# Loading attention inputs four heads at a time, spreading the loads over a group's steps, and reordering the last output tiles

## The chip, the cores and the metric

The kernel runs on one core of one Trainium2 chip, in one launch. The metric is the device time of that launch in microseconds (us), as the median of several runs. One further execution was taken with the hardware profiler; all rows below are from it.

## The reference, cut to what matters

Inputs are float32: local queries, keys and values of 4 batches, 8 heads, 512 positions and head size 64, and 32 global rows per head. Global rows attend to everything; a local row attends to the 32 global rows and to local rows at most 32 positions away. Two feed-forward nets over 2176 tokens follow.

```python
k_all = concat([k_g, k_l], axis=2); v_all = concat([v_g, v_l], axis=2)
out_g = sm(scale * q_g @ k_all.T) @ v_all
s_ll  = where(abs(pos[:, None] - pos[None, :]) <= 32, scale * q_l @ k_l.T, -1e9)
out_l = sm(concat([scale * q_l @ k_g.T, s_ll])) @ v_all
x = concat([out_g, out_l], axis=2)           # to [2176, 512]
h = x @ w_in;  x = (h * cos(h)) @ w_out      # 512 -> 2048 -> 512
h = relu(x @ w2_in);  out = (h * h) @ w2_out
```

## The kernel before, in words

**Attention.** Heads are taken in pairs, pair p from 0 to 15 (four pairs to a batch). Two pairs make a group of four heads, group gi from 0 to 7. A group is five items: two halves of 256 rows for each of its two pairs (class Local, line 400) and the 128 global rows of its four heads (class Global, line 526). There are 40 items, and the program is written by hand as a pipeline of steps (the loop at line 896). In step s item s has its scores made on TensorE (`S`, lines 405 and 530), its softmax on VectorE and ScalarE (`SM`, lines 421 and 546), one step later its reciprocal and normalisation (`RC`, `NM`), two steps later the transposes of its weights (`TM`, lines 476 and 591), and at lags 3 and 4 their evacuation and the product with the values (`TE`, `OM`, lines 483, 492, 606). Within a step the stages are emitted in the order of `CFG["order"]` (line 26); `CFG["lag"]` (line 28) says how many steps behind its item each is.

Before an item can start, its pair's keys and queries are transposed on TensorE: `TRK` (line 321) three steps ahead, `TRQ` (line 359) two steps ahead. `KEV` (line 334, ScalarE) and `KC` (line 348, GpSimd) evacuate and copy the keys. The last 32 keys of all heads are loaded once as `ktn`, transposed at `prep_ktail` (line 380), and copied in by `KC`.

**Loads.** Every load is issued by hand on the SyncE queue (SP in the rows), except the first queries and `ktn`, which ScalarE issues (lines 630 to 635). Per pair there are four transfers of keys (`load_k`, line 265), two of queries (`load_q`, line 280), five of values (`load_v`, line 290, into the ring `VA`), and two that copy the values, shifted by 64 rows, from `VA` to `VB` within SBUF (`copy_v`, line 307). In DRAM each row of a head is 64 floats, so these loads consist of 256-byte pieces. `LK`, `LQ`, `LV` and `CV` in the order place them for pair p + 2. Queue instructions run in order: one that must wait for a tile holds up all behind it. In `OM` the first product with `VB` waits for the second copy.

**Weights.** The float32 weights are split into a high and a low part. `Feed` (line 164) loads a block of 512 KB on SP (`conv_load`, line 119), and three, four and five steps later ScalarE, VectorE and GpSimd each do a part of the conversion (`conv_a`, `conv_b`, `conv_c`). A credit of 0.35 per step in which it is allowed paces it; in attention it starts a block at steps 3, 8, 13 and so on, five steps apart.

**Feed-forward.** `ffn_step` (line 856) makes one block of 128 hidden features for up to 512 tokens per step: three products per pair of operands (high by high, low by high, high by low), first into `h` (`g1`, line 746), then three steps later into `y` (`g2`, line 764). Sums over groups of hidden blocks are kept in `ypart`. In the last group of the second net `y_evac` (line 784) adds `y` and `ypart` into a fresh tile `osb` of two buffers, and `store` (line 804) writes it out: one transfer for a tile of local rows, four for the tile of global rows, which is the very last one.

```python
            elif c in ("LK", "LQ", "LV", "CV"):
                p = due(L[c])
                if p is not None and p + 2 < B * NPAIR:
                    dict(LK=load_k, LQ=load_q, LV=load_v, CV=copy_v)[c](p + 2)
```

Of the kernel before, what the change touches and what calls it, by code (L numbers as in the profile page):

```python
# [40 lines left out]
         'LK': -2,  # L41
         'LQ': 0,
         'LV': 3,
         'CV': 6},
# [18 lines left out]
def kernel(  # L63
# [100 lines left out]
    class Feed:  # L164


        def __init__(self):
            self.jobs = [(g, q) for g in range(2 * NC) for q in range(2)]
            self.stage = [None] * 6
            self.credit = 0.0  # L170
            self.nsplit = 0
            self.done = 0
            self.half = None

        def begin(self, rate):

            self.credit = min(self.credit + rate, 2.0)
            job = None
            if self.credit >= 1.0 and self.jobs:
                g, q = self.jobs[0]  # L180
                if g < self.nsplit + NR:
                    job = self.jobs.pop(0)
                    conv_load(*job)
                    self.credit -= 1.0
            self.stage = [job] + self.stage[:-1]
            a, b, c = self.stage[3:]
            if a:
                conv_a(*a)
            return conv_b(*b) if b else []

        def end(self):
            c = self.stage[5]
            if c:
                conv_c(*c)
                self.done += 1
# [59 lines left out]
    VA = [lp.tile([P, 5, 2, D], F32, name=f"va{i}") for i in range(4)]  # L255
    VB = [lp.tile([P, 4, 2, D], F32, name=f"vb{i}") for i in range(4)]
# [8 lines left out]
    def load_k(p):  # L265
        b, kk = divmod(p, NPAIR)
        h0 = 2 * kk
        t = ep.tile([P, 4, 2, D], F32, tag="kn", name="kn", bufs=2)
        nc.sync.dma_start(t[0:SG, 0], k_g[b, h0 : h0 + 2].rearrange("h p d -> p h d"))
        nc.sync.dma_start(  # L270
            t[SG:P, 0], k_l[b, h0 : h0 + 2, 0 : P - SG].rearrange("h p d -> p h d")
        )
        kn[p] = t
        for h in range(2):
            nc.sync.dma_start(
                t[:, 1:4, h],
                k_l[b, h0 + h, P - SG : SL - SG].rearrange("(c p) d -> p c d", p=P),
            )

    def load_q(p, queue=nc.sync):  # L280
        b, kk = divmod(p, NPAIR)
        h0 = 2 * kk
        u = ep.tile([P, 4, 2, D], F32, tag="qn", name="qn", bufs=2)
        for h in range(2):
            queue.dma_start(
                u[:, :, h], q_l[b, h0 + h].rearrange("(c p) d -> p c d", p=P)
            )
        qn[p] = u

    def load_v(p):  # L290
        b, kk = divmod(p, NPAIR)
        h0 = 2 * kk
        va = VA[p % 4]
        nc.sync.dma_start(va[0:32, 0], v_g[b, h0 : h0 + 2].rearrange("h p d -> p h d"))
        nc.sync.dma_start(
            va[32:128, 0], v_l[b, h0 : h0 + 2, 0:96].rearrange("h p d -> p h d")
        )
        for h in range(2):
            nc.sync.dma_start(  # L299
                va[:, 1:4, h],  # L300
                v_l[b, h0 + h, 96:480].rearrange("(c p) d -> p c d", p=P),
            )
        nc.sync.dma_start(
            va[0:32, 4], v_l[b, h0 : h0 + 2, 480:512].rearrange("h p d -> p h d")
        )

    def copy_v(p):
        va, vb = VA[p % 4], VB[p % 4]
        nc.sync.dma_start(vb[0:64], va[64:128, 0:4])
        nc.sync.dma_start(vb[64:128], va[0:64, 1:5])  # L310
# [10 lines left out]
    def tr_k(p):  # L321
        b, kk = divmod(p, NPAIR)
        tk = bank(BT, "tk")
        for c in range(4):
            nc.tensor.transpose(  # L325
                tk[:, c * P : (c + 1) * P],
                kn[p][:, c].rearrange("p h d -> p (h d)"),
                ident,
            )
        t = ep.tile([P, 8, KTB], F32, tag="kT", name="kT", bufs=3)  # L330
        kT[p] = t
        tks[p] = tk
# [15 lines left out]
    def k_copy(p):  # L348
        b, kk = divmod(p, NPAIR)
# [7 lines left out]
        nc.gpsimd.tensor_scalar(t[:, 7, 64:128], ktail[:, kk, b, :], **one)  # L357

    def tr_q(p):
        tq = bank(BT, "tq")  # L360
        for c in range(4):
            nc.tensor.transpose(  # L362
                tq[:, c * P : (c + 1) * P],
                qn[p][:, c].rearrange("p h d -> p (h d)"),
                ident,
            )
# [33 lines left out]
    class Local:  # L400
# [91 lines left out]
        def o_mm(self):  # L492
            self.o = bank(BO, "o")[:, 0:256].rearrange("p (i q) -> p i q", i=2)
            for i in range(2):
# [9 lines left out]
                for half in range(2):  # L504
                    v = (VB if half else VA)[self.p % 4]
                    q = slice(64 * half, 64 * half + 64)
                    for h in range(2):
                        nc.tensor.matmul(  # L508
                            self.o[64 * h : 64 * h + 64, i, q],
                            lhsT=v[:, 2 * self.hb + i, h, :],  # L510
# [15 lines left out]
    class Global:  # L526
# [79 lines left out]
        def o_mm(self):  # L606
            self.o = bank(BO, "og")[:, 0 : 2 * SG].rearrange("p (i q) -> p i q", i=2)
            for i in range(2):
                va = VA[(self.b * NPAIR + 2 * self.g + i) % 4]
                for c in range(5):  # L610
                    for h in range(2):
# [4 lines left out]
                            lhsT=va[0:r, c, h, :],  # L616
# [13 lines left out]
    load_q(0, nc.scalar)  # L630
    load_k(0)
# [4 lines left out]
    load_k(1)  # L636
    load_q(1)
# [125 lines left out]

    def g2(s):
# [3 lines left out]
        ne = NK if net == 0 else n // P  # L768
        if c_first:
            yps[:] = [bank(BY, "y") for e in range(ne)]  # L770
        for e in range(ne):
# [12 lines left out]
    def y_evac(s):  # L784
        net, first, last, (c0, n), _, _, _ = steps[s]
        for e, y in enumerate(yps):
# [17 lines left out]
    def store(t, osb):  # L804
        if t * P < NLOC:
            b, j = divmod(t * P, SL)
            r0 = b * (SL + SG) + SG + j
            nc.sync.dma_start(out[r0 : r0 + P, :], osb)
        else:
            for b in range(B):  # L810
                r0 = b * (SL + SG)
                nc.sync.dma_start(out[r0 : r0 + SG, :], osb[SG * b : SG * b + SG, :])
# [83 lines left out]
    for s in range(L["TRK"], NI + L["OE"]):  # L896
        due = lambda k: due_tr.get(s - k)
        cb, qe = [], []
        for c in CFG["order"]:
# [7 lines left out]
            elif c in ("TRK", "TRQ", "KEV", "KC", "QE"):  # L907
# [21 lines left out]
            elif c in ("LK", "LQ", "LV", "CV"):  # L929
                p = due(L[c])  # L930
                if p is not None and p + 2 < B * NPAIR:
                    dict(LK=load_k, LQ=load_q, LV=load_v, CV=copy_v)[c](p + 2)
            else:
# [3 lines left out]
                if c == "S":  # L937
                    i.s_mm()
                    if s == 0:
                        small = prep_qg()  # L940
                elif c == "SM":
                    for op in i.softmax():
                        op()
                    if s == 0:
# [5 lines left out]
                else:  # L950
                    dict(NM=i.norm, TM=i.t_mm, TE=i.t_evac, OM=i.o_mm, OE=i.o_evac)[c]()
        if s == 0:
            load_v(1)
        if s == 1:
            copy_v(1)
# [13 lines left out]
    open_pool("y", "o", "w2")  # L969
# [40 lines left out]
```

## Time and profile before

| what | value |
|---|---|
| median of 3 runs (lowest to highest) | 923.08 us (921.78 to 923.24) |
| the profiled execution: its time | 922.14 us |
| its span, first to last instruction | 920.4 us |
| TensorE (PE) busy | 888.4 us, 97% of the span |
| VectorE (DVE) / ScalarE (ACT) / GpSimd (POOL) busy | 489.8 / 473.3 / 407.1 us |
| moved by DMA | 57.09 MB |

The span lies 1.7 us below the time of its own execution, which lies 0.9 us below the median. "Idle before" in a row is the time for which an engine stood still ahead of an instruction, and the name behind the arrow is what ended it. PEclk is the granted TensorE clock as a share of full speed (1.0 is the 2.4 GHz level, 0.5 the 1.2 GHz level).

### The profile page before, as it was taken

The page shows a single profiled execution, that of the slowest core. Times are in us where ns is not written, and L with a number is a line of the kernel's source. Part 1 is how long each engine was busy: PE and PEld are TensorE (multiplying, and loading weights), DVE is VectorE, ACT ScalarE, POOL GpSimd, SP SyncE. Part 2 cuts the span into 40 slices and gives each one's busy share as a digit, 9 for nine tenths or more (in the row PEclk, how much of TensorE's full clock was granted, in tenths as well). Part 3 has the DMA queues.
Part 4 walks back from the last instruction along what each step waited for, and adds up shares of the span by engine and source line. Part 5 has one row for each costly group of instructions (what it writes and reads, how often), then busy time and mean ns, then how long its engine had stood idle before and what let it go on. Part 6 is the DMA issues. An engine that isn't in the chain of part 4 may idle for free.

```text
span 920.4 us, 15407 instructions
## 1 busy us (share of the span) xinstructions
PE 888.4 (97%) x5696; PEld 792.5 (86%) x5696; DVE 489.8 (53%) x1049; ACT 473.3 (51%) x1096; POOL 407.1 (44%) x458
## 2 busy tenths in 40 slices
PE   4898989999999999999999999999999999999997
PEld 3677767999999999999999988888989888889995
DVE  3666868667767566864565484433423733222221
ACT  3777878667665655665455464343333632222221
POOL 4555766455554434653333464333423652222221
PEclk9999999999999999999999999999999999999999
DMA  6576574211212121221211021112100101010001
GB/s 134 136 179 148 142 178 127 68 57 47 69 46 69 47 59 35 67 69 47 69 47 50 20 69 46 47 47 69 47 1 1 46 1 46 1 46 1 35 35 35
DMA packets 84106, 57.09 MB, mean 62 GB/s; under 512 B 59328, under 2 KB 75712, under 8 KB 84032
## 3 DMA queue, kind: packets, MB, share of 16 engines
q1 hardware_dynamic: 81888, 55.59, 21.5%
q8 instruction: 45, 0.74, 0.3%
q10 hardware_dynamic: 2144, 0.52, 0.3%
q14 instruction: 29, 0.24, 0.1%
HBM read 47.45 MB, written 4.46 MB: 56 GB/s over the span
## 4 chain that ended last, share of the span: by engine, by line
PE 91%; SPq 3%; DMA 3%; ACT 1%; POOL 1%; issue 1%; DVE 0%; ACTq 0%; POOLq 0%; DVEq 0%
PE h L754 41%; PE y L778 41%; PE s L412 2%; PE o L496 1%; PE o L508 1%; PE tw L480 1%; DMA vb<-va 1%; PE tk L325 1%; PE og L614 1%; DMA kn<-in_k_l_dram 1%; SPq L316 1%; PE tq L362 1%; PE sg L538 1%; DMA raw<-in_moe_w_in_dram 1%; SPq L299 0%
## 5 line engine op out<-in xcount | busy, mean ns | idle before, releaser
L754 PE MATMUL h<-x,w 128*128 128x436 f32 (+3 forms) x1920 | 404.2, 359 | 0.0
L849 POOL TENSOR_TENSOR glo<-cr,ghi 128x436 fp32r<-128x436 f32 (+3 forms) x160 | 189.7, 1186 | 438.9 <-ACT ghi L843 380.7
L754 PEld LDWEIGHTS h<-x,w 128*128 128x128 f32 x1920 | 354.6, 188 | 28.2
L778 PE MATMUL y<-ghi,w 128*128 128x436 f32 (+1 forms) x640 | 178.1, 359 | 0.0
L778 PE MATMUL y<-w,ghi 128*128 128x512 f32 x544 | 168.4, 390 | 0.0
L838 DVE TENSOR_TENSOR cr<-h,cr 128x436 f32<-128x436 f32 (+3 forms) x160 | 96.5, 604 | 128.8 <-ACT cr L829 115.0
L742 DVE TENSOR_TENSOR x<-xt,x 128x436 fp32r<-128x436 f32 (+3 forms) x100 | 103.1, 1040 | 98.2 <-ACT x L741 83.2
L829 ACT ACTIVATE cr<-h 128x384 f32<-128x384 f32 (+1 forms) x80 | 42.7, 534 | 201.3 <-PE h L754 200.2
L778 PEld LDWEIGHTS y<-ghi,w 128*128 128x128 f32 x640 | 120.3, 188 | 6.5
L778 PEld LDWEIGHTS y<-w,ghi 128*128 128x128 f32 x544 | 101.4, 188 | 18.9
L778 PE MATMUL y<-glo,w 128*128 128x436 f32 (+1 forms) x320 | 115.1, 360 | 0.0
L778 PE MATMUL y<-w,glo 128*128 128x512 f32 x272 | 106.8, 393 | 0.0
L823 ACT ACTIVATE ck<-h 128x436 int32<-128x436 f32 (+1 forms) x80 | 42.6, 532 | 107.1 <-PE h L754 107.1
L843 ACT ACTIVATE ghi<-cr 128x436 fp32r<-128x436 f32 (+3 forms) x160 | 89.7, 560 | 14.8 <-DVE cr L838 13.4
L825 DVE SCALAR_TENSOR_TENSOR cr<-h,ck 128x436 f32<-128x436 f32 (+1 forms) x80 | 48.6, 608 | 90.7 <-ACT ck L823 90.7
L162 POOL TENSOR_TENSOR r<-cu,cc 128x512 uint32<-128x512 uint32 x64 | 92.2, 1441 | 3.2 <-DVE cc L152 3.2
L741 ACT ACTIVATE x<-xt 128x436 fp32r<-128x436 f32 (+3 forms) x100 | 55.1, 559 | 19.5 <-PE h L754 19.2
L778 PEld LDWEIGHTS y<-glo,w 128*128 128x128 f32 x320 | 60.1, 188 | 2.9
L778 PEld LDWEIGHTS y<-w,glo 128*128 128x128 f32 x272 | 51.0, 188 | 10.7
L834 ACT ACTIVATE cr<-cr,halfpi 128x436 f32<-128x436 f32 (+1 forms) x80 | 52.5, 656 | 13.0 <-DVE cr L825 13.0
L438 ACT ACTIVATE pt<-pt,st 128x160 f32<-128x160 f32 x128 | 53.0, 419 | 4.3 <-DVE st L428 4.3
L152 DVE SCALAR_TENSOR_TENSOR cc<-raw,cc 128x512 uint32<-128x512 uint32 x64 | 54.7, 855 | 0.0
(90 smaller groups left out, 876.2 us busy)
## 6 DMA issues: line engine op xcount, KB each, us to landing
raw<-in_moe_w_in_dram SPq DMA_DIRECT2D x32, 512.0 KB, 3.7
raw<-in_moe_w_out_dram SPq DMA_DIRECT2D x32, 512.0 KB, 3.4
vb<-va SPq DMA_DIRECT2D x32, 128.0 KB, 2.7
out_dram<-osb SPq DMA_DIRECT2D x16, 256.0 KB, 2.0
qn<-in_q_l_dram SPq DMA_DIRECT2D x30, 128.0 KB, 3.0
kn<-in_k_l_dram SPq DMA_DIRECT2D x32, 96.0 KB, 2.7
va<-in_v_l_dram SPq DMA_DIRECT2D x32, 96.0 KB, 3.2
kn<-in_k_l_dram SPq DMA_DIRECT2D x16, 48.0 KB, 2.4
```

Source lines behind the costliest of these rows:

```text
L152: lambda: v.scalar_tensor_tensor(c, t[:, :, 1].bitcast(U32), 0x80000000, c, op0=ALU.bitwise_and, op1=ALU.bitwise_or,),
L162: nc.gpsimd.tensor_tensor(ring[g][:, q, :].bitcast(U32), u, c, op=ALU.add)
L438: nc.scalar.activation(self.pt[:, u, :], self.pt[:, u, :], AF.Exp, bias=self.st[:, 0, u : u + 1], scale=-1.0, accum_out=self.st[:, 1, u : ...
L741: nc.scalar.activation(hi, xr, AF.Copy)
L742: return lambda: (nc.vector if kk in XD else nc.gpsimd).tensor_tensor(lo, xr, hi.bitcast(F32), op=ALU.subtract)
L754: nc.tensor.matmul(h, lhsT=w[:, ws, 0, kk * P : (kk + 1) * P], rhs=x, start=(k == 0), stop=(k == 3 * NK - 1),)
L778: nc.tensor.matmul(o, lhsT=l, rhs=r, start=(c_first and k == 0), stop=(c_last and k == 2))
L825: lambda: nc.vector.scalar_tensor_tensor(r, h, INV2PI, k, op0=ALU.mult, op1=ALU.subtract),
L834: nc.scalar.activation(ctmp[s], ctmp[s], AF.Sin, bias=halfpi, scale=TWOPI)
L838: nc.vector.tensor_tensor(r, hps.pop(s), r, op=ALU.mult)
L843: nc.scalar.activation(ghi[s], ctmp[s], AF.Copy)
L849: nc.gpsimd.tensor_tensor(lo, ctmp.pop(s), hi.bitcast(F32), op=ALU.subtract)
```

## The change

Keys, queries and values are loaded for a group of four heads in a transfer, not for two heads (one of the first group excepted). Per group that is 5, 4 and 6 transfers and 2 copies, where it was 8, 4, 10 and 4 for its two pairs. The rings hold two groups in place of two pairs (keys, queries) or four pairs (values). Loads are placed for group gi + 2 in the steps 5gi (keys), 5gi + 1 (queries), 5gi + 8 (values) and 5gi + 11 (copies). The first group's queries are eight transfers on ScalarE's queue, ahead of `ktn`. `prep_ktail`, the tail copy and the later constants of pair 0 move behind its query transposes; `prep_qg` moves from step 0 to step 2. The weight pipeline is one stage shorter: ScalarE's part runs two steps behind the load. In the last group of the second net the sum is made in `ypart` itself and stored from there, and the last block's tiles are computed, added and stored in reverse.

```diff
-         'LK': -2, 'LQ': 0, 'LV': 3, 'CV': 6},
+         'LK': 0, 'LQ': 1, 'LV': 8, 'CV': 11},
...
-            self.stage = [None] * 6
+            self.stage = [None] * 5
...
-            self.credit = min(self.credit + rate, 2.0)
+            self.credit = min(self.credit + rate, 1.5)
...
-            a, b, c = self.stage[3:]
+            a, b, c = self.stage[2:]
...
-    VA = [lp.tile([P, 5, 2, D], F32, name=f"va{i}") for i in range(4)]
-    VB = [lp.tile([P, 4, 2, D], F32, name=f"vb{i}") for i in range(4)]
+    VA = [lp.tile([P, 5, 4, D], F32, name=f"va{i}") for i in range(2)]
+    VB = [lp.tile([P, 4, 4, D], F32, name=f"vb{i}") for i in range(2)]
...
+    def load_k(gi, sub=4):
+        b, h0 = gi // 2, 4 * (gi % 2)
+        t = ep.tile([P, 4, 4, D], F32, tag="kn", name="kn", bufs=2)
+        kn[gi] = t
+        for i in range(0, 4, sub):
+            d, g = slice(i, i + sub), slice(h0 + i, h0 + i + sub)
+            nc.sync.dma_start(t[0:SG, 0, d], k_g[b, g].rearrange("h p d -> p h d"))
+            for c in range(4):
+                r0 = SG if c == 0 else 0
+                nc.sync.dma_start(
+                    t[r0:P, c, d],
+                    k_l[b, g, P * c - SG + r0 : P * c + P - SG].rearrange("h p d -> p h d"),
+                )
+    def load_q(gi, queue=nc.sync, sub=4):
...
+            for c in range(4):
+                queue.dma_start(
+                    u[:, c, d], q_l[b, g, P * c : P * c + P].rearrange("h p d -> p h d")
+                )
+    def load_v(gi):
...
+    def copy_v(gi):
+        va, vb = VA[gi % 2], VB[gi % 2]
         nc.sync.dma_start(vb[0:64], va[64:128, 0:4])
         nc.sync.dma_start(vb[64:128], va[0:64, 1:5])
...
-    load_q(0, nc.scalar)
-    load_k(0)
+    load_q(0, nc.scalar, 2)
+    load_k(0, 2)
...
-    load_k(1)
-    load_q(1)
+    load_v(0)
...
+    def tiles(s):
+        net, _, _, (c0, n), _, _, _ = steps[s]
+        e = list(range(NK if net == 0 else n // P))
+        return e[::-1] if c0 + n == NT and s > NS - 20 else e
...
-                part = ypart[1][:, c0 // P + e, :]
-                dst = pools["o"].tile([P, DM], F32, tag="osb", name="osb", bufs=2) if last else None
+                part = dst = ypart[1][:, c0 // P + e, :]
...
                 elif c == "KC":
-                    if p == 0:
-                        prep_ktail()
                     k_copy(p)
-                    if p == 0:
-                        later_constants()
-                        load_v(0)
-                        load_vg(0)
-                        copy_v(0)
                 elif c == "QE":
                     for op in qe:
                         op()
+                    if p == 0:
+                        prep_ktail()
+                        k_tail(0)
+                        later_constants()
             elif c in ("LK", "LQ", "LV", "CV"):
                 p = due(L[c])
-                if p is not None and p + 2 < B * NPAIR:
-                    dict(LK=load_k, LQ=load_q, LV=load_v, CV=copy_v)[c](p + 2)
+                if p is not None and p % 2 == 0 and p // 2 + 2 < 2 * B:
+                    dict(LK=load_k, LQ=load_q, LV=load_v, CV=copy_v)[c](p // 2 + 2)
...
-                    if s == 0:
+                    if s == 2:
                         small = prep_qg()
...
+        if s == -2:
+            load_k(1)
+            load_vg(0)
+        if s == -1:
+            load_q(1)
         if s == 0:
+            copy_v(0)
+        if s == 2:
             load_v(1)
-        if s == 1:
+        if s == 5:
             copy_v(1)
```

## Rows read from the trace of the kernel before

**Rows 1.** Windows: busy us per engine, granted clock, DMA share, GB/s.

```profile
core 0: us, PE busy (x) PEld busy (x) DVE busy (x) ACT busy (x) POOL busy (x), PEclk, DMA share, GB/s
...
24.00:160.00 136.00, 122.56 (x1856) 98.50 (x1855) 97.78 (x453) 107.33 (x388) 86.33 (x180) 0.97 0.62 151
160.00:912.00 752.00, 752.00 (x3735) 684.38 (x3735) 381.04 (x550) 356.39 (x679) 309.34 (x244) 1.00 0.14 43
```

**Rows 2.** Waits of TensorE up to 165 us: total, times, longest.

```profile
PE o L508 <- DMA vb<-va: 9.7, 4, 3.6
```

**Rows 3.** Chain that ended last, before the third of these waits: start, us, what.

```profile
105.79 0.26 PE o L508 x8
106.05 0.54 SPq L269
...
114.33 2.37 DMA vb<-va
```

**Rows 4.** Windows of 2 us around the second wait, columns as in rows 1.

```profile
78.00:80.00 2.00, 1.02 (x14) 0.65 (x10) 1.59 (x6) 0.75 (x4) 1.52 (x5) 1.00 0.35 83
80.00:82.00 2.00, 0.43 (x6) 0.46 (x8) 0.29 (x2) 0.00 (x0) 1.45 (x4) 0.80 0.85 197
```

**Rows 5.** Timeline of TensorE: global scores and the next item's first scores.

```profile
41.28 1.19 PE L538 MATMUL sg<-kT,qgbd 128*64 128x320 f32 x8
...
49.21 0.52 PE L412 MATMUL s<-kT,qT 64*64 64x160 f32 x1
...
97.44 1.19 PE L538 MATMUL sg<-kT,qgbd 128*64 128x320 f32 x8
...
100.59 0.48 PE L412 MATMUL s<-kT,qT 64*64 64x160 f32 x2
```

**Rows 6.** Issues on SP by source line: ns min/median/max, first and last start us.

```profile
L275 SPq DMA_DIRECT2D kn<-in_k_l_dram x32: 384/455/493, 1.6 to 126.4; - x32
...
L285 SPq DMA_DIRECT2D qn<-in_q_l_dram x30: 368/532/1650, 5.2 to 132.5; - x30
```

**Rows 7.** Window of 2 to 10 us, columns as in rows 1.

```profile
2.00:10.00 8.00, 1.58 (x5) 0.95 (x6) 1.43 (x5) 1.88 (x2) 2.16 (x8) 1.00 0.94 195
```

**Rows 8.** Timeline of the start: ScalarE's issues, first scores, first weight transposes.

```profile
0.72 1.04 ACTq L285 DMA_DIRECT2D qn<-in_q_l_dram  x2
...
1.79 5.10 ACTq L633 DMA_DIRECT2D ktn<-in_k_l_dram  x4
...
12.65 0.88 PE L412 MATMUL s<-kT,qT 64*64 64x160 f32 x16
...
16.82 1.25 PE L412 MATMUL s<-kT,qT 64*64 64x160 f32 x16 [1.57 <-DVE qT L368]
...
20.06 0.87 PE L325 MATMUL tk<-ident,kn 128*128 128x128 f32 x3 [1.17 <-DMA kn<-in_k_l_dram]
...
20.73 1.06 PE L480 MATMUL tw<-ident,pt 128*128 128x128 f32 x4
```

**Rows 9.** First weight block: its transfer on the chain, its conversion on ScalarE.

```profile
28.61 5.05 DMA raw<-in_moe_w_in_dram
...
33.69 0.68 ACT L142 ACTIVATE cu<-raw 128x512 f32<-128x512 f32 x1 [0.83 <-DMA raw<-in_moe_w_in_dram]
```

**Rows 10.** Costliest groups: GpSimd's part of a weight conversion.

```profile
L162 POOL TENSOR_TENSOR r<-cu,cc 128x512 uint32<-128x512 uint32 x64 | 92.2, 1441 | 3.2 <-DVE cc L152 3.2
```

**Rows 11.** Timeline of the end: last additions and stores.

```profile
912.16 1.37 DVE L796 TENSOR_TENSOR osb<-y,ypart 128x512 f32<-128x512 f32 x2 [5.70 <-PE y L778]
...
912.88 1.01 SPq L808 DMA_DIRECT2D out_dram<-osb  x2
...
915.03 0.69 DVE L796 TENSOR_TENSOR osb<-y,ypart 128x512 f32<-128x512 f32 x1 [1.50 <-DMA out_dram<-osb]
915.75 1.75 SPq L812 DMA_DIRECT2D out_dram<-osb  x4
```

More of the change, by code (lines that the diff above doesn't have):

```diff
@@ L40 @@
          'OE': 4,
[L41 to L44, printed above, removed]
+         'LK': 0,
+         'LQ': 1,
+         'LV': 8,
+         'CV': 11},
  'ndv': 1,
@@ L191, in end @@
         def end(self):
-            c = self.stage[5]
+            c = self.stage[4]
             if c:
@@ L263 @@
     kn, qn, kT, qT, tks = {}, {}, {}, {}, {}
[L265 to L274, printed above, removed]
+    def load_k(gi, sub=4):
[11 more added lines that the diff above has]
+                )
@@ new lines, in load_q @@
+    def load_q(gi, queue=nc.sync, sub=4):
+        b, h0 = gi // 2, 4 * (gi % 2)
+        u = ep.tile([P, 4, 4, D], F32, tag="qn", name="qn", bufs=2)
+        qn[gi] = u
+        for i in range(0, 4, sub):
+            d, g = slice(i, i + sub), slice(h0 + i, h0 + i + sub)
+            for c in range(4):
[3 more added lines that the diff above has]
+    def load_v(gi):
+        b, h0 = gi // 2, 4 * (gi % 2)
+        va, g = VA[gi % 2], slice(h0, h0 + 4)
+        nc.sync.dma_start(va[0:SG, 0], v_g[b, g].rearrange("h p d -> p h d"))
+        for c in range(5):
+            r0, r1 = (SG if c == 0 else 0), (SG if c == 4 else P)
@@ L275, in load_k @@
             nc.sync.dma_start(
-                t[:, 1:4, h],
-                k_l[b, h0 + h, P - SG : SL - SG].rearrange("(c p) d -> p c d", p=P),
-            )
[L280 to L305, printed above, removed]
@@ L348, in k_copy @@
     def k_copy(p):
-        b, kk = divmod(p, NPAIR)
         t = kT[p]
@@ L356, in k_copy, with k_tail @@
             )
-        nc.gpsimd.tensor_scalar(t[:, 7, 64:128], ktail[:, kk, b, :], **one)
+        if p:
+            k_tail(p)
+    def k_tail(p):
+        b, kk = divmod(p, NPAIR)
+        nc.gpsimd.tensor_scalar(
+            kT[p][:, 7, 64:128], ktail[:, kk, b, :], 1.0, 1.0, op0=ALU.mult, op1=ALU.mult
+        )
     def tr_q(p):
@@ L504, in o_mm @@
                 for half in range(2):
-                    v = (VB if half else VA)[self.p % 4]
+                    v = (VB if half else VA)[self.p // 2 % 2]
                     q = slice(64 * half, 64 * half + 64)
@@ L767, in g2 @@
         hi, lo = gt.pop(s)
-        ne = NK if net == 0 else n // P
         if c_first:
-            yps[:] = [bank(BY, "y") for e in range(ne)]
-        for e in range(ne):
+            yps[:] = [bank(BY, "y") for e in tiles(s)]
+        for e in tiles(s):
             sl = slice(e * P, (e + 1) * P)
@@ L785, in y_evac @@
         net, first, last, (c0, n), _, _, _ = steps[s]
-        for e, y in enumerate(yps):
+        for e in tiles(s):
+            y = yps[e]
             if net == 0:
@@ L802, in y_evac, with store @@
                 store(c0 // P + e, dst)
-    def store(t, osb):
+    def store(t, y):
         if t * P < NLOC:
@@ L807, in store @@
             r0 = b * (SL + SG) + SG + j
-            nc.sync.dma_start(out[r0 : r0 + P, :], osb)
+            nc.sync.dma_start(out[r0 : r0 + P, :], y)
         else:
@@ L811, in store @@
                 r0 = b * (SL + SG)
-                nc.sync.dma_start(out[r0 : r0 + SG, :], osb[SG * b : SG * b + SG, :])
+                nc.sync.dma_start(out[r0 : r0 + SG, :], y[SG * b : SG * b + SG, :])
     def act_a(s):
@@ L968 @@
     late.close()
-    open_pool("y", "o", "w2")
+    open_pool("y", "w2")
     y = pools["y"].tile([P, NK * NT], F32, name="ypart")
```

16 lines of the change are left out of this document (8 added, 8 removed).

## The prediction, made before the changed kernel ran

> **What bounds the kernel now.** I read the windows by stage first. From 160 to 912 us TensorE is busy in all of 752 us [rows 1]: nothing that the change does to loads can shorten that stretch, and the feed-forward part stays as it is. From 24 to 160 us, the attention, TensorE is busy for 122.56 of 136 us, at a mean granted clock of 0.97 [rows 1]. So 13.4 us are idle, and 0.03 of 136 us, about 4.1 us (3.4 to 4.8 by the rounding), are lost to the 1.2 GHz level. Next I asked for TensorE's waits: 9.7 us in four pieces, the longest 3.6 us, are for the second copy of the values into `VB` [rows 2]. What made the copy late is in the chain. Before the third wait it leaves TensorE at 106.05 us and runs along SP's queue, issue behind issue, until the copy at 114.33 us [rows 3]: the copy waited its turn, not for its data. The windows around the second wait say the same of the DMA engines: from 78 to 80 us, when TensorE begins to stand, they are busy to 0.35 only [rows 4]. After such a wait the clock falls (0.80 in the next window, [rows 4]), which costs again. The pace without a wait is in the timeline: from the global scores to the next item's scores 3.15 us (97.44 to 100.59), against 7.93 us with the longest wait (41.28 to 49.21) [rows 5]. I call 3.15 us a step.
>
> **Fewer issues.** By the code SP issues 64 transfers of keys, 30 of queries, 80 of values and 32 copies, 206 in all. After the change it is 45 (40, and 5 more as the first group comes in halves), 28, 48 and 16, so 137. At the median issue of 0.455 us [rows 6], 69 issues fewer take 31 us off a queue that works through the whole of attention. An issue of four heads for 128 rows has 512 pieces. A query transfer of before has as many, at a median of 0.532 us [rows 6], so the new issues cost about what the old ones did. The copies also move: values two and a half to three steps ahead of the copy, the copy three steps ahead of the first product that needs it. At 3.15 us a step that is over 9 us for a landing of 2.37 us [rows 3]; a copy of twice the size might take twice that, and still fits. In the steady part the keys and queries come seven steps ahead. The four waits should therefore go, with the clock that they cost: 9.7 + 3.4 = 13.1 us (the lower end of the clock's loss, as some of it will have other causes). The pair of timeline rows agrees: 7.93 - 3.15 = 4.8 us for a wait of 3.6. Ends: 9.7 if no clock comes back, 13.4 + 4.1 = 17.5 if every idle moment goes. ScalarE is what is late next, with 107.33 us busy of 136 [rows 1]; with 13 us taken out it is at 87%, still below TensorE.
>
> **The start.** Here the change costs. In the first 2 to 10 us the DMA engines are busy to 0.94 [rows 7], and ScalarE, which must issue its own loads before it can evacuate the first keys, needs 5.10 us for four transfers of 64 KB after 1.04 us for two of 128 KB [rows 8]. After the change it issues twelve of 64 KB. Five at 0.5 us and seven at 1.28 us (5.10 / 4) make 11.5 us, so it is free at 12.2 instead of 6.9 us, 5.3 us later. The first scores depend on `ktn`, issued last; but the query transposes now stand ahead of the tail, which gives back about 0.9 us on TensorE, so they start near 17.0 instead of 12.65 us. From there to the first weight transposes before needs 8.1 us (12.65 to 20.73), of which 1.57 us wait for query copies queued behind the global queries' copies, and 1.17 us for keys [rows 8]; both causes are moved away, so 2.7 us come back. Net 1.7 us by this path.
>
> A second path runs over SP. Ahead of the first weight block it had 44 issues and now has 50, and the data are 1.6 MB more, as whole groups are loaded. Six issues are 2.7 us; the block landed at 33.66 us (28.61 + 5.05), where ScalarE had waited 0.83 us for it in step 6 [rows 9]. Now ScalarE wants it in step 5, one step sooner. If it lands as before, the pipeline is one step late there, 3.15 us; if it lands 2.7 us later, 5.9 us. SP also waited in before for memsets and for landings, part of which goes. I take 4.0 us for the whole start, the middle of the second path, which is the later one. Ends: a gain of 1 us if issues flow freely on both queues (the two waits of 2.7 us go and 1.7 us of the rest remains), and 8 us lost if the block lands at 38.5 us.
>
> **Edits costed at nothing.** The credit's cap of 1.5 changes no start of a block: 0.35 per allowed step never reaches it in attention, and in the feed-forward part TensorE has no gap to lose. GpSimd's part of a conversion, 1.44 us [rows 10], now falls into a step in which it also copies keys; its 86.33 busy us in 136 [rows 1] leave it room over two steps. Without that room it would cost 1.44 us for each of eight blocks, 11.5 us. The reverse order wants, for its first tile, the bank that the block before evacuates first; TensorE fills `h` meanwhile, so the price is nothing, and one addition of 0.69 us [rows 11] without that cover. Moving `prep_qg` to step 2 puts its copies ahead of nothing urgent before step 4.
>
> **The end.** Before, the third addition waited 1.50 us for a buffer, began at 915.03, and four stores of 0.44 us followed, the last issued at 917.06; the span ends 3.3 us after that. Now the tile with four stores is first: additions follow each other from 912.16 and end at 914.24, the four stores are issued from 912.88 to 914.63, the two others (0.50 us each [rows 11]) behind them, the last at 915.13. With 3.3 us behind it, and 0.3 us more as the last store is of 256 KB, the end is 918.8: 1.6 us earlier. Ends: 1.2 and 2.2.
>
> **Sum.** Against the profiled execution's own 922.14 us: 922.14 - 13.1 + 4.0 - 1.6 = 911.4. The median of the runs stands 0.94 us above that execution, so I predict 912.4 us.
>
> A rule that speaks against this: the Trainium skill, page "DMA: Bandwidth & Descriptors", section "Issuing engines are not separate DMA queues", says that the time a sequencer takes to initiate a DMA is usually small beside the DMA itself. By it fewer issues would gain little, the first rival below. The share of 0.35 disagrees for this stretch [rows 4].
>
> **Rivals.**
> (a) The transfers set the pace, or an issue grows with its pieces. The bytes and the 256-byte pieces stay the same, and the DMA share over attention is 0.62 [rows 1], which speaks for it; the idle DMA engines before the copies speak against it. Then the waits stay and only the end gains: 922.1 - 1.6 + 0.9 = 921.4. Chance 0.06.
> (b) The weight blocks come too late all through. ScalarE's part now stands two steps, 6.3 us, behind the issue, and a block took 5.05 us [rows 9]: if SP is more than 1.25 us behind its step, ScalarE waits, and softmax behind it, up to a step of 3.15 us for each of eight blocks, 25.2 us: 911.4 + 25.2 + 0.9 = 937.5, slower than before. At 1.3 us per block the gain of 10.7 us is gone. For it: SP ran late in before. Against it: SP has 31 us less to issue. Chance 0.06.
> (c) The start costs nothing or gives 1 us: 922.1 - 13.1 - 1 - 1.6 + 0.9 = 907.3. For it: the waits of 2.7 us. Against it: the 5.10 us for four issues [rows 8]. Chance 0.16.
>
> **Numbers.** The forecast has the remaining 0.72. The range holds the forecast with its ends (13.1 less or more by 3.4, the start by up to 4, the end by 0.5) and (c): 905 to 919. A difference of 0.2%, 1.85 us, is what a measurement of this kernel can tell from none. Faster by more: forecast, (c) and a little of (b), 0.90. Within: (a) and a mild (b), 0.05. Slower: 0.05.
>
> **What would show it.** Right: no wait of TensorE for `VB` after 30 us, SP's queue with gaps in attention, a granted clock near 1.0 there, the first scores near 17 us, one wait of ScalarE for the first weight block, the first feed-forward product some 9 us earlier, no wait ahead of the last additions. Wrong: waits for `VB` that stay, waits of ScalarE for weight blocks in every group, or TensorE standing for GpSimd's normalisation in the third step of a group.

## The result and the profile after

The changed kernel took 915.02 us, the median of 4 runs (913.74 to 915.77); the kernel before, measured beside it, 923.16 us. The ratio is 0.9912, with a 95% interval of 0.9894 to 0.9929: 8.1 us faster, where 10.7 were forecast. The direction, the range (905 to 919) and the main cause were right, the size was 2.6 us too hopeful. Measured once more beside the kernel before (experiment 9), the changed kernel is 10.0 us faster.

The profiled execution took 915.77 us, the highest of its four. From the page of the changed kernel, span and busy time:

```profile
span 914.0 us, 15267 instructions
...
PE 888.2 (97%) x5696; PEld 791.6 (87%) x5696; DVE 492.8 (54%) x1049; ACT 473.1 (52%) x1096; POOL 406.8 (45%) x456
```

TensorE's work is the same 888 us. The span is 6.4 us shorter (920.4 to 914.0), and all of it is idle time or clock. The windows by stage of the changed kernel (busy us per engine, granted clock, DMA share, GB/s) say where:

```profile
24.00:160.00 136.00, 127.40 (x1904) 101.61 (x1902) 103.87 (x454) 110.61 (x395) 89.79 (x182) 0.97 0.64 149
...
24.00:50.00 26.00, 21.39 (x290) 17.26 (x286) 15.62 (x72) 15.09 (x58) 13.00 (x31) 0.87 0.86 180
50.00:141.30 91.30, 89.26 (x1448) 71.24 (x1447) 74.31 (x347) 80.54 (x301) 65.02 (x138) 1.00 0.67 158
```

Against [rows 1], TensorE is busy for 127.40 of the 136 us instead of 122.56. From 50 us to the last global scores it is idle for 2 us in 91 at full clock: little is left to gain in the steady part. What is left stands at its two ends, 4.6 idle us and a clock of 0.87 before 50 us, and a slow last step from 141 to 148 us.

TensorE's waits of the changed kernel up to 165 us, and from the same view for SP's queue (total, times, longest):

```profile
PE o L510 <- DMA vb<-va: 2.6, 1, 2.6
...
SPq L295 <- PE og L616: 21.4, 6, 8.3
```

Where [rows 2] had four waits for `VB`, there is one, at 27.92 us, in the first group. SP now stands six times at the head of a group's values until TensorE has done with the old ones, for 21.4 us in all: the queue has gaps, its issues are no longer behind.

The step from the global scores to the next scores, in the timeline of the changed kernel on TensorE, answers to [rows 5]:

```profile
46.86 1.19 PE L540 MATMUL sg<-kT,qgbd 128*64 128x320 f32 x8
...
50.01 0.48 PE L414 MATMUL s<-kT,qT 64*64 64x160 f32 x2
...
141.28 1.19 PE L540 MATMUL sg<-kT,qgbd 128*64 128x320 f32 x8
...
148.41 2.62 PE L755 MATMUL h<-x,w 128*128 128x436 f32 x12
```

The last step of attention in the same timeline of the kernel before:

```profile
147.53 1.19 PE L538 MATMUL sg<-kT,qgbd 128*64 128x320 f32 x8
...
153.17 2.62 PE L754 MATMUL h<-x,w 128*128 128x436 f32 x12
```

The step that lasted 7.93 us before [rows 5] is 3.15 us (46.86 to 50.01). The others that had waited, each timed in the same way in both traces, went from 7.30 to 3.15, from 5.47 to 3.60 and from 4.85 to 3.72 us. The four give 4.78 + 4.15 + 1.87 + 1.13 = 11.9 us. Yet the third group's first scores start at 50.01, not 4.78 us earlier than 49.21, which would be 44.43: the start became 5.6 us longer. And from the last global scores to the first feed-forward product it is 7.13 us, where it was 5.64 (147.53 to 153.17). The whole account: -11.9 (waits) + 0.1 (the other steps) + 5.6 (start) + 1.5 (last step of attention) - 0.1 (feed-forward) - 1.6 (end) = -6.4 us.

**The start.** Timeline of the changed kernel, ScalarE's issues, TensorE, SP and ScalarE's conversion:

```profile
0.72 4.74 ACTq L288 DMA_DIRECT2D qn<-in_q_l_dram  x8
5.67 3.35 ACTq L635 DMA_DIRECT2D ktn<-in_k_l_dram  x4
...
14.09 1.34 PE L414 MATMUL s<-kT,qT 64*64 64x160 f32 x16
...
27.92 0.34 PE L510 MATMUL o<-tws,vb 128*64 128x64 f32 x4 [2.64 <-DMA vb<-va]
...
29.93 0.43 SPq L125 DMA_DIRECT2D raw<-in_moe_w_in_dram  x1
...
35.13 0.69 ACT L142 ACTIVATE cu<-raw 128x512 f32<-128x512 f32 x1 [3.39 <-DMA raw<-in_moe_w_in_dram]
...
38.73 0.28 PE L600 MATMUL tlg<-ident,ptg 128*32 128x128 f32 x1 [1.97 <-ACT tgs L492]
```

ScalarE is free at 9.0 us, and the first scores come at 14.09 us, 1.4 us later than in [rows 8]. By the first weight transposes (21.20 against 20.73) the delay is 0.5 us. The cost comes after that, through SP's order: the copies to `VB` stand behind the global values, the second group's queries and the third group's keys, and TensorE waits 2.64 us; the first weight block stands behind the third group's queries and the second group's values, and ScalarE waits 3.39 us for it, with TensorE's next transposes 1.97 us behind that. After each of TensorE's two waits the clock falls (0.50 in 30 to 32 and in 40 to 42 us, the 1.2 GHz level); over 24 to 50 us it is 0.87.

**The last step of attention.** GpSimd (POOL) and VectorE (DVE) in the timeline of the changed kernel:

```profile
142.49 0.62 DVE L151 TENSOR_SCALAR cu<-cu 128x512 uint32<-128x512 uint32 x1
...
144.53 1.26 POOL L162 TENSOR_TENSOR r<-cu,cc 128x512 uint32<-128x512 uint32 x1
144.58 1.24 DVE L560 TENSOR_TENSOR stg<-stg 128x1 f32<-128x1 f32 x1
```

The same instruction in the kernel before:

```profile
149.58 0.16 DVE L558 TENSOR_TENSOR stg<-stg 128x1 f32<-128x1 f32 x1
```

Two things hold up the global softmax on VectorE. VectorE's own part of a weight conversion (lines 151 and 152, 1.2 us together) now stands ahead of it, so that its first reduction begins 2.49 us after the global scores, where it was 1.23 us. Then an instruction on one element per partition takes 1.24 us instead of 0.16, and ends at 145.82, just after GpSimd's addition of the weight conversion (145.79); in the kernel before that addition was already over. Together VectorE is 2.3 us late, and the step is 1.5 us longer. By the code the missing pipeline stage puts both parts of the conversion one step sooner, into this place; experiment 1 puts the stage back.

**The end.** VectorE (DVE) and SP in the timeline of the changed kernel:

```profile
907.33 2.05 DVE L802 TENSOR_TENSOR ypart<-y,ypart 128x512 f32<-128x512 f32 x3 [5.70 <-PE y L784]
908.04 1.75 SPq L818 DMA_DIRECT2D out_dram<-ypart  x4
909.89 0.88 SPq L814 DMA_DIRECT2D out_dram<-ypart  x2
```

The wait of [rows 11] is gone, the four stores go first, and from the first addition to the end of the span it is 6.67 us instead of 8.24: 1.6 us, as forecast.

### The profile page after: what moved, and what is told of

Its sections match the earlier page's. It is cut to its first block, busy times and chain, and to the rows that moved or that the text cites. A ratio compares the mean times of both kernels' runs of the same rounds, so it can differ in the third digit from the quotient of the medians.

```text
span 914.0 us, 15267 instructions
## 1 busy us (share of the span) xinstructions
PE 888.2 (97%) x5696; PEld 791.6 (87%) x5696; DVE 492.8 (54%) x1049; ACT 473.1 (52%) x1096; POOL 406.8 (45%) x456
## 3 DMA queue, kind: packets, MB, share of 16 engines
q1 hardware_dynamic: 78736, 55.33, 22.0%
## 4 chain that ended last, share of the span: by engine, by line
PE 93%; ACT 2%; DMA 2%; DVE 1%; SPq 1%; POOL 0%; issue 0%; ACTq 0%; POOLq 0%
PE h L755 41%; PE y L784 41%; PE s L414 2%; PE tw L482 1%; PE o L498 1%; PE og L616 1%; PE o L510 1%; ACT pt L440 1%; PE tk L321 1%; PE tq L364 1%; PE sg L540 1%; DMA qn<-in_q_l_dram 1%; DMA raw<-in_moe_w_in_dram 1%; ACT w L225 0%; DMA va<-in_v_l_dram 0%; SPq L298 0%
## 5 line engine op out<-in xcount | busy, mean ns | idle before, releaser
L743 DVE TENSOR_TENSOR x<-xt,x 128x436 fp32r<-128x436 f32 (+3 forms) x100 | 97.7, 986 | 96.8 <-ACT x L742 81.8
L840 ACT ACTIVATE cr<-cr,halfpi 128x436 f32<-128x436 f32 (+1 forms) x80 | 52.5, 656 | 11.9 <-DVE cr L831 11.8
L152 DVE SCALAR_TENSOR_TENSOR cc<-raw,cc 128x512 uint32<-128x512 uint32 x64 | 56.7, 885 | 0.0
```

Of the source, the lines that this page charges most:

```text
L152: lambda: v.scalar_tensor_tensor(c, t[:, :, 1].bitcast(U32), 0x80000000, c, op0=ALU.bitwise_and, op1=ALU.bitwise_or,),
L743: return lambda: (nc.vector if kk in XD else nc.gpsimd).tensor_tensor(lo, xr, hi.bitcast(F32), op=ALU.subtract)
L840: nc.scalar.activation(ctmp[s], ctmp[s], AF.Sin, bias=halfpi, scale=TWOPI)
```

## The experiments

Each is the changed kernel with one edit, unless it says otherwise. The kernel before ran on the same chip each time, and each ratio is against it.

**1. The sixth pipeline stage back (stage6).** Does the shorter weight pipeline cost what the start and the last step lost?

```diff
-            self.stage = [None] * 5
+            self.stage = [None] * 6
...
-            self.credit = min(self.credit + rate, 1.5)
+            self.credit = min(self.credit + rate, 2.0)
...
-            a, b, c = self.stage[2:]
+            a, b, c = self.stage[3:]
...
-            c = self.stage[4]
+            c = self.stage[5]
```

> The changed kernel with the weight pipeline back at six stages and a credit cap of 2.0; the loads and the end stay as changed. Theory: the shorter pipeline costs time at two places of the changed kernel, ScalarE's wait of 3.4 us for the first weight block in step 5 (with the clock that TensorE loses behind it), and 1.5 us between the last global scores and the first feed-forward product (7.13 us, 5.64 before), where VectorE's part of a conversion now stands ahead of the global softmax. Then that wait falls below 1 us, the second stretch goes back to about 5.7 us, and the time is 3 to 5 us below the changed kernel: 910 to 912 us. Rival: the first block is late because SP issues it late, whatever the step, and the second stretch is long for another reason: then under 1.5 us are gained and the time stays at 914 to 915 us.

912.10 us beside 925.08, ratio 0.9856 (0.9838 to 0.9874). Timeline (TensorE, ScalarE, GpSimd and VectorE) and window of this kernel:

```profile
36.40 0.67 ACT L142 ACTIVATE cu<-raw 128x512 f32<-128x512 f32 x1 [1.16 <-DMA raw<-in_moe_w_in_dram]
...
47.15 0.48 PE L414 MATMUL s<-kT,qT 64*64 64x160 f32 x2
...
137.17 1.28 POOL L162 TENSOR_TENSOR r<-cu,cc 128x512 uint32<-128x512 uint32 x1
137.24 1.68 DVE L743 TENSOR_TENSOR x<-xt,x 128x436 fp32r<-128x436 f32 x1 [0.56 <-ACT x L742]
...
138.46 0.76 PE L540 MATMUL sg<-kT,qgbd 128*64 128x320 f32 x4
...
144.97 2.23 PE L755 MATMUL h<-x,w 128*128 128x436 f32 x10
...
24.00:152.00 128.00, 120.47 (x1858) 95.71 (x1857) 99.09 (x455) 107.61 (x388) 87.59 (x183) 1.00 0.68 155
```

The wait for the block shrinks from 3.39 to 1.16 us, though the block was issued later (31.09 against 29.93): one more step of patience, as the theory has it. The third group's scores come at 47.15 instead of 50.01. By the ratios (0.9895 and 0.9912 for the two measurements of the changed kernel) the stage is worth 3.6 to 5.2 us, and removing it was a loss, not nothing. At the second place both delays of the softmax are gone: the small instruction takes 0.16 us again, and VectorE's part of the conversion comes behind the softmax. From the first product behind the global scores to the first feed-forward product it is 4.97 us, against 6.11 in the changed kernel and 4.62 before. Yet the whole last step is 6.5 us (138.46 to 144.97), shorter than 7.13 but not the 5.64 of before: here GpSimd's addition of the block before began 0.07 us ahead of another VectorE instruction, line 743, which took 1.68 us (0.69 in the kernel before, line 742), and TensorE waited 0.33 us in the middle of the global scores.

**2. Two heads in a transfer again, in the new places (sub2).** The same places and order, the same bytes and 256-byte pieces; only the number of transfers differs, 248 of keys, queries, values and copies on SP by the code, for 137. (By the pages of the two profiles SP's queue moves 55.33 MB in both; its packets are 80512 for 78736, which is 16 more for each added issue.) `load_k` and `load_q` take `sub=2`, and `load_v` gets the same loop:

```diff
-    def load_k(gi, sub=4):
+    def load_k(gi, sub=2):
...
-    def load_q(gi, queue=nc.sync, sub=4):
+    def load_q(gi, queue=nc.sync, sub=2):
...
+        for i in range(0, 4, 2):
+            d, g = slice(i, i + 2), slice(h0 + i, h0 + i + 2)
+            nc.sync.dma_start(va[0:SG, 0, d], v_g[b, g].rearrange("h p d -> p h d"))
...
```

> The changed kernel with every load of keys, queries and values split in two transfers of two heads, in the same places; the copies stay whole. SP then has about 248 issues, more than the 206 before. Theory (the number of issues on SP made the copies late): at 0.455 us each they take 113 us of the queue, waits of TensorE for VB come back with several us in total, and the time rises by 4 us or more, to 919 us or above. Rival (where the loads stand in the program made the copies late, not their number): no wait for VB outside the first group, and a time within 1.5 us of the changed kernel's 915 us.

948.21 us beside 925.08, ratio 1.0248 (1.0227 to 1.0269). Waits up to 165 us, window and chain of this kernel:

```profile
ACT cu L142 <- DMA raw<-in_moe_w_in_dram: 10.5, 3, 7.9
PE o L512 <- DMA vb<-va: 16.8, 4, 7.6
...
24.00:152.00 128.00, 99.27 (x1417) 79.30 (x1419) 72.42 (x339) 76.25 (x286) 62.51 (x137) 0.88 0.57 133
...
87.27 0.42 SPq L300
...
95.84 0.47 SPq L307
96.35 3.95 DMA vb<-va
```

This run decides between transfers and issues. From 87.27 to 96.31 us the chain is SP issuing without a pause, then the copy, then TensorE, as in [rows 3] but longer. The DMA share is 0.57, where the changed kernel has 0.67 in the same window, while by the ratios the kernel is 31 us slower than the changed one ((1.0248 - 0.9912) x 925). So neither bytes nor pieces set the pace, but the number of issues. The rule quoted in the prediction is that the time to initiate a DMA is usually small beside the DMA itself (the Trainium skill, page "DMA: Bandwidth & Descriptors", section "Issuing engines are not separate DMA queues"). The trace agrees for one issue, 0.47 us beside 3.95 us for the copy; but 16 other issues stand in a row ahead of it here, 8.6 us, and of such a sum the rule says nothing. The waits for weight blocks also show rival (b)'s mechanism: it appears when SP is late.

**3. The first group's copies early (copy0).** The two copies move from step 0 to step -2, ahead of the global values, and `later_constants` sets `VA` before `VGZ`:

```diff
...
             load_k(1)
+            copy_v(0)
             load_vg(0)
...
-        if s == 0:
-            copy_v(0)
```

> The changed kernel with the first group's copies of values issued ahead of the global values, of the second group's queries and the third group's keys, and the memset that they need made first. Theory: TensorE's wait of 2.64 us for VB at 27.9 us is a matter of SP's order alone and goes; but the first weight block is then what the start waits for, as it is issued no earlier, so that most of it comes back as a longer wait of ScalarE for that block (3.4 us now, 5 to 6 us then), and the time falls by under 1.5 us: 913.5 to 915 us. Rival: the two waits are in series, and all 2.6 us and the clock behind them are gained: 911 to 912.5 us.

916.08 us beside 925.08, ratio 0.9897 (0.9875 to 0.9920): no gain. On ScalarE in its timeline:

```profile
36.10 0.66 ACT L142 ACTIVATE cu<-raw 128x512 f32<-128x512 f32 x1 [6.11 <-DMA raw<-in_moe_w_in_dram]
```

The wait for `VB` is gone, but the next one is longer: ScalarE's wait for the block grew from 3.39 to 6.11 us, and TensorE's behind it from 1.97 to 5.39 us. The theory expected this.

**4. Half of the first queries on SP (actq).** Frees ScalarE earlier, which was the prediction's first path.

```diff
-    def load_q(gi, queue=nc.sync, sub=4):
+    def load_q(gi, queue=nc.sync, sub=4, part=(0, 4)):
...
-    load_q(0, nc.scalar, 2)
+    load_q(0, nc.scalar, 2, (0, 2))
     load_k(0, 2)
+    load_q(0, nc.sync, 2, (2, 4))
```

> The changed kernel with the second half of the first group's queries on SP behind the keys, so that ScalarE issues eight transfers and not twelve. Theory: the keys' first evacuation and the tail transposes wait for ScalarE's queue; ScalarE is free near 6 us instead of 9.0 and the first scores start at 11 to 12 us instead of 14.1. What follows is set by SP's queue, so the first weight block lands no earlier (35.1 us), and the time changes by under 1.5 us. Rival: the start is one chain from ScalarE's queue to the end, and 2 to 3 us are gained: 912 to 913 us.

916.58 us beside 925.08, ratio 0.9896 (0.9872 to 0.9921). The first scores start at 11.69 us instead of 14.09, and nothing comes of it: TensorE then waits for keys, queries and `VB` (2.31 us), ScalarE for the block (3.14 us), and the third group's scores start at 50.51 us. The first scores do not set the pace of the start.

**5. The old end (oldtail).** A fresh `osb` tile of two buffers and the order of before:

```diff
-        return e[::-1] if c0 + n == NT and s > NS - 20 else e
+        return e
...
-                part = dst = ypart[1][:, c0 // P + e, :]
+                part = ypart[1][:, c0 // P + e, :]
+                dst = pools["o"].tile([P, DM], F32, tag="osb", name="osb", bufs=2) if last else None
...
```

> The changed kernel with the end as it was: fresh tiles for the last sums, tiles in forward order. Theory: the end is worth 1.6 us by itself: from the beginning of the last products to the end of the span 15.1 us as before, against 13.6 us in the changed kernel, and no other stretch differs by more than 0.5 us beyond the start's scatter. Rival: the in-place sums also freed VectorE inside the second net, so that some of the feed-forward stretch is longer too and 3 us or more are lost.

916.00 us beside 925.73, ratio 0.9896 (0.9869 to 0.9922). Timeline of this kernel, span 916.3 us:

```profile
908.36 1.37 DVE L803 TENSOR_TENSOR osb<-y,ypart 128x512 f32<-128x512 f32 x2 [5.70 <-PE y L784]
911.21 0.69 DVE L803 TENSOR_TENSOR osb<-y,ypart 128x512 f32<-128x512 f32 x1 [1.48 <-DMA out_dram<-osb]
```

The wait for a buffer is back, 1.48 us, and from the first addition to the end it is 7.94 us instead of 6.67: by the two profiles the new end is worth 1.3 us. The ratio can't show it, since the intervals of this and of the changed kernel overlap; the start alone scatters by more (below).

**6. The first weight block ahead of the second group's values (rawfirst).**

```diff
-        if s == 2:
+        if s == 3:
             load_v(1)
```

> The changed kernel with the second group's values loaded at the end of step 3 and not of step 2, so that the first weight block goes ahead of them on SP; five stages as changed. Theory: ScalarE's wait for that block (3.4 us) is a matter of what stands ahead of it on SP: with six issues fewer it is issued near 26.5 us and lands near 32 us, the wait falls to 0.5 us or less, the clock behind it comes back, and the first scores of the third group start 2 to 4 us earlier (50.0 us now); 911 to 913 us. Rival: the block needs its 5 us of landing because the DMA engines are full, and going first moves the same wait to the values: the start does not change by more than 1 us.

912.12 us beside 925.73, ratio 0.9856 (0.9841 to 0.9870). ScalarE and TensorE in its timeline:

```profile
32.72 0.68 ACT L142 ACTIVATE cu<-raw 128x512 f32<-128x512 f32 x1 [1.42 <-DMA raw<-in_moe_w_in_dram]
...
46.04 0.48 PE L414 MATMUL s<-kT,qT 64*64 64x160 f32 x2
```

One load moved behind another in SP's order gives as much as the sixth stage did: the wait for the block is 1.42 us instead of 3.39 and the third group's scores come 4 us sooner, in an execution whose clock is 1.00 in 24 to 50 us (what the clock alone can do there, experiment 9 shows).

**7. Three together (best2): stage6, copy0 and rawfirst.** If the waits form a chain, each behind the other, removing them together pays where copy0 alone did not.

> Three edits together: six stages, the first group's copies early, the first weight block ahead of the second group's values. Theory: the waits of the start are one chain over SP; with the copies early TensorE does not wait for VB, and with the block early and wanted in step 6 ScalarE does not wait either. The third group's first scores start near 44.5 us (50.0 in the changed kernel, 47.2 with six stages alone), and the time is 5 to 6 us below the changed kernel, 909 to 910 us on a chip where that takes 915. Rival: another wait takes their place, the second group's values or queries, and it is no better than six stages alone.

908.91 us beside 925.73, ratio 0.9822 (0.9808 to 0.9837): the best version of this study, faster than both kernels. Its timeline and window:

```profile
32.46 0.69 ACT L142 ACTIVATE cu<-raw 128x512 f32<-128x512 f32 x1
...
43.73 0.48 PE L414 MATMUL s<-kT,qT 64*64 64x160 f32 x2
...
24.00:50.00 26.00, 25.46 (x401) 20.50 (x404) 20.29 (x105) 22.00 (x82) 17.04 (x41) 1.00 0.88 188
```

Neither wait is left, TensorE is idle for 0.5 us in 26, and the third group's scores start at 43.73 us: 5.5 us earlier than before the change, which is the 4.78 us of the stall and 0.7 more. The start's cost has gone, here and in the second profile of this kernel (42.50 us, experiment 10).

**8. best2 and the queries of actq (best3).**

> As the one before, with the second half of the first group's queries on SP, so that ScalarE is free sooner. Theory: by itself that moved the first scores from 14.1 to 11.7 us and was given back at SP's transfers; with the later waits gone it counts for 1 us or less, as the second group's keys and queries then land just when they are wanted. Rival: it now counts in full, 2.4 us below the kernel with three edits.

912.12 us beside 925.73, ratio 0.9859 (0.9842 to 0.9875): some 3 us worse than best2, which neither theory had. From its timeline on TensorE and its windows:

```profile
23.23 0.70 PE L365 MATMUL tq<-ident,qn 128*128 128x128 f32 x2 [2.11 <-ACT pt L441]
25.02 0.95 PE L365 MATMUL tq<-ident,qn 128*128 128x128 f32 x2 [1.09 <-DMA qn<-in_q_l_dram]
...
46.47 0.48 PE L415 MATMUL s<-kT,qT 64*64 64x160 f32 x2
...
24.00:37.00 13.00, 11.68 (x146) 8.73 (x146) 6.64 (x33) 7.43 (x26) 3.48 (x10) 0.87 0.88 201
```

TensorE starts early (first scores at 11.42 us) and then stands in short waits up to 26 us, the last two of 2.11 and 1.09 us; the clock is 0.87 in 24 to 37 us, where best2 has 1.00. The third group's scores come 2.7 us later than in best2, which is the difference. That the waits brought the clock down fits the other traces, but was not tried by itself.

**9 and 10. The changed kernel and best2 again, on one chip (changed_again, best2_again).**

> The changed kernel once more, as it is, beside the best version on one chip. Both theories: a ratio of 0.99 to before, within the scatter of its first timing.

> The kernel with three edits once more. Theory: 5 to 7 us below the changed kernel on the same chip. Rival: part of its lead was the chip's, and it is under 3 us below.

914.88 and 908.41 us beside 924.87, ratios 0.9895 (0.9879 to 0.9912) and 0.9823 (0.9808 to 0.9838): both repeat, 6.5 us apart. The changed kernel's window and timeline show something else:

```profile
24.00:50.00 26.00, 20.70 (x326) 16.39 (x325) 16.20 (x77) 17.42 (x67) 14.90 (x37) 1.00 0.90 195
...
47.75 0.48 PE L414 MATMUL s<-kT,qT 64*64 64x160 f32 x2
```

TensorE's waits are the same (2.65 us for `VB`, 2.12 us behind the block), and ScalarE's for the block is 2.78 us, 0.6 less than in the first profile; but the clock is 1.00 in 24 to 50 us, and the third group's scores come at 47.75 instead of 50.01 us. So about 2.3 of the 5.6 us that the start cost in the first profile do not come in each execution, and most of that is the clock's.

**11. The copies three steps later (cv14).** The same issues as the changed kernel, but a group's copies then stand behind the next group's values in SP's order.

```diff
-         'CV': 11},
+         'CV': 14},
```

> The changed kernel with the copies of values three steps later in the program, so that on SP they stand behind the next group's values, which wait for TensorE; the number of issues and all sizes stay. Theory (a copy is late through what stands ahead of it on SP): it is then issued behind a wait for the global product of the step before its use and six issues, about 4 us late; TensorE waits 3 to 5 us for VB in each of six groups, and the time rises by 18 us or more with the clock. Rival (only the number of issues on SP counted): no change beyond 2 us.

951.24 us beside 924.87, ratio 1.0278 (1.0255 to 1.0302). TensorE's waits up to 165 us and SP's timeline:

```profile
PE o L510 <- DMA vb<-va: 26.8, 6, 5.9
...
85.37 2.96 SPq L298 DMA_DIRECT2D va<-in_v_l_dram  x5
88.37 0.47 SPq L305 DMA_DIRECT2D vb<-va  x1
```

The copies are issued right behind values that had to wait until TensorE was done with the old ones, and TensorE waits for them in six groups. The time rises by 36 us, twice the least that was expected. So fewer issues alone do not do it: the place of the copies, which the change also moved, matters as much. How much of this loss is the shorter lead and how much the values ahead, this run does not part. Nor do experiments 2 and 11 say what part of the gain over the kernel before is the count's and what part the place's: one has more issues than that kernel, the other a place that it did not have, and fewer issues in the old places were not tried.

## Why the prediction was right in the main and off in size

- **The waits for `VB` go: right.** They were SP's, by count (experiment 2) and by order (11). The term was 13.1 us and measured 11.9: two of the four steps that had waited became 3.15 us, but the others 3.60 and 3.72. Beside the 9.7 us of the waits only 2.2 came back, not 3.4. The step that was off is "with the clock that they cost", said of all four waits. In the trace of before they last 3.57, 2.55, 2.09 and 1.47 us, and the clock is 0.84 and 0.81 around the first two (41 to 50 and 77 to 86 us), but 1.00 around the last two (110 to 122 and 130 to 140 us). The first two steps gave 8.9 us for 6.1 us of wait, the last two 3.0 us for 3.6: there no clock came back, and some of the wait had covered other work.
- **An issue of twice the heads costs about the same: right.** In the changed kernel, issues of keys and queries on SP (ns least, median, most):

```profile
L276 SPq DMA_DIRECT2D kn<-in_k_l_dram x36: 313/472/987, 1.2 to 98.8; - x36
...
L288 SPq DMA_DIRECT2D qn<-in_q_l_dram x28: 385/592/1529, 17.1 to 106.0; - x28
```

  472 and 592 ns, against 455 and 532 in [rows 6]. Rival (a) has fallen with this and with experiment 2.
- **The start: the right path, and a size that differs between executions.** The term was +4.0 and measured +5.6; the second profile of the changed kernel (experiment 9) makes it +3.3 by the same reckoning. So that 4.0 lies between them is in part luck. The text calls 4.0 the middle of a path whose two ends it gives as 3.15 and 5.9; that middle is 4.5. The step that failed on the first path was that ScalarE would be free at 12.2 us and the first scores come near 17: seven issues were priced at 1.28 us each, from a row in which four took 5.10 us, but the twelve took 4.74 + 3.35 us, and ScalarE was free at 9.0. On the second path the step was right in kind (the block is wanted one step sooner, by a ScalarE that waits 3.39 us), but two things were left out: the first group's own copies, which the change put behind other loads (2.64 us), and the clock. Rival (c), a free start, was wrong for this change; experiment 7 shows that it was within reach.
- **Edits costed at nothing: wrong for the shorter pipeline.** For the conversion's new place the prediction asked only whether GpSimd has room. It has; but VectorE's part came to stand ahead of the last softmax (1.3 us), and GpSimd's addition held up an instruction of that softmax (1.1 us). The step became 1.5 us longer, a term that the sum didn't have; it comes in both profiles of the changed kernel, and with the stage back the delays of the softmax are gone (experiment 1). The stage as a whole is worth 3.6 to 5.2 us (experiment 1); between the first profile and that of experiment 1, 2.9 us of it are at the start.
- **The end: right**, 1.6 us between the profiled executions of before and after, 1.3 in experiment 5.
- **The sum.** Against the profiled execution the forecast was 911.4 and the measurement 915.77: 1.2 from the waits, 1.6 from the start, 1.5 from the last step make 4.3 of the 4.4 us. The medians are only 2.6 us apart, since the profiled execution is 0.75 us above the median this time, and was 0.94 below it before; that closeness is chance. What comes in both profiles of the changed kernel are the 1.2 us of the waits and the 1.5 us of the last step.
- **Signs that did not come.** The first feed-forward product came 4.8 us earlier (153.17 to 148.41), not some 9; the first scores came at 14.09 us, not near 17; and the clock over the whole of attention stayed at 0.97, as it is 0.87 up to 50 us and 1.00 from there.
- **Rival (b)**, late weight blocks throughout, did not come: only the first block was late. Experiment 2 shows that such waits come when SP is behind.

## What to carry to other kernels

Treat a DMA queue as an engine: count its issues, multiply by the time of one, and look at what stands ahead of the transfer that somebody waits for; the DMA engines may be little busy while the queue is full. When a pipeline is shortened, the first item pays, because its load has no slack yet: compare its landing with the step that now wants it. And waits at a start follow each other, so one that is removed alone may only lengthen the next; take the chain away together, then measure.

## What the runs showed of the hardware beyond that

- A VectorE instruction on one element per partition with two inputs (line 560, a maximum) took 1.24 us beside a GpSimd addition of two tiles of 128x512, where its median is 0.16 us, and ended 0.03 us after it. The Trainium skill, page "SBUF — State Buffer", section "Who interferes with whom", says that a VectorE instruction with two inputs in SBUF contends with a GpSimd instruction that reads SBUF. The same page of the Trainium skill, section "Summary: rules for kernel authors", says that the second of the two to issue is blocked until the first finishes. The trace agrees with both: the two inputs of line 560 lie in SBUF, GpSimd began 0.05 us earlier, and the end of the one follows the end of the other. In all eight traces with five pipeline stages the instruction took 1.23 to 1.24 us at this place; in the five with six stages it never took more than 0.37 us. No run changed this place alone.
- The granted clock did not answer to the same waits in the same way: with nearly equal waits of TensorE before 39 us (2.64 and 1.97 us, 2.65 and 2.12 us), it was 0.87 in 24 to 50 us in one execution of the changed kernel and 1.00 in another. The third group's scores came 2.3 us apart. A single profile of a start with waits therefore tells the waits, but not the time that they cost. Why the clock fell in one and not in the other stays open.
